# A decode step with two cached-attention layers: tiles of two heads with 64 KB rows in three fixed places, and VectorE's products stored before they are summed

## The chip, the cores and the metric

The kernel runs on one core of one Trainium2 chip. The metric is the device time of one execution in microseconds. The kernel before took 2550.75 us in the median of three runs (2548.57 to 2551.07).

## What is computed

Two tokens (batch 2, one position each, width 576) pass twice through an attention block and a mixer block, with the same weights both times. In the attention 32 heads of width 128 meet a cache of 16,384 keys and values per head and batch row; all numbers are bf16.

```python
q = (x @ wq).reshape(B, Sq, H, Dh) ...
scores = jnp.einsum("bhqd,bhkd->bhqk", q, k_cache) * (Dh ** -0.5)
p = _softmax(scores, axis=-1)
o = jnp.einsum("bhqk,bhkd->bhqd", p, v_cache)
return o... @ wo
...
x = x + _A_ref(_layernorm(x, axis=-1), A_k_cache, A_v_cache, A_wq, A_wo)
x = x + _B_ref(_layernorm(x, axis=-1), B_w1, B_w2, B_w3, B_w4)
x = x + _A_ref(_layernorm(x, axis=-1), A_k_cache, A_v_cache, A_wq, A_wo)
x = x + _B_ref(_layernorm(x, axis=-1), B_w1, B_w2, B_w3, B_w4)
```

With one position the shifts in the mixer read padding only, so `@ w2` multiplies zeros. Nearly all bytes are the caches: 64 pairs of batch row and head, each with 4 MiB of keys and 4 MiB of values, are read once per layer, except a few that stay on the chip between the layers.

## The kernel before, in words

**Tiles.** A unit `u` is one head of one batch row (64 units per layer). Its keys are one tile, its values another: 128 partitions by 32,768 bytes, that is 128 positions per partition, one contiguous run of 32 KB per partition (`plan_tile`). SBUF holds six such places (`NSLOT`, `TILE`), which the tiles of K and V take in a ring. In front of them lie 6,144 bytes for three transposed chunks (`AUX`) and a small gap (`EXTRA`).

**Order of the transfers.** `plan_all` lists every load of the program in one order: K of unit 0, the weights wq and w2, then K and V alternating (V one unit behind K), then the weights of the tail of layer 0 cut to fit a window of freed bytes (`WINDOW`), then layer 1 alike. All loads are issued by SyncE (SP) in that order; `Store.pump` issues the next as soon as the program has released all the bytes that it overwrites, and SP waits (L98, L182) for the engines' semaphores that say so. A tile's bytes are released 512 at a time (`used`), but a whole tile is loaded by one DMA, so the last reader of the old tile decides. When a tile has landed, GpSimd passes the news to TensorE and VectorE (`landed`; POOLq L187 in the profile).

**One unit.** Of a unit's 128 blocks of 128 keys, 64 go to TensorE and 64 to VectorE (`PB`). TensorE takes eight blocks at a time (`CH`): it transposes them into one of four PSUM banks (`transposed`, L1255), ScalarE copies the bank to SBUF (`evacuate`, L1270), and two chunks later (`LEAD`) TensorE multiplies the eight transposed blocks by the query column (`scores`, L1285). VectorE multiplies 16 blocks by the query spread over all partitions into `prod` and sums them at once (`dots`, L1315 and L1319), four times per unit. Then come the maxima (L1324, L1330, L1332), a maximum over the partitions on GpSimd (L1335), two exponentials with their sums (L1345, L1349), and 128 matmuls of the values with the probabilities, which accumulate one column (`pv`, L1375).

**The loop.** In `attention` a loop's turn is three units (`NS`), 21 turns per layer. Within a unit `s` the engines also do the maximum and the exponentials of unit `s-1` and its `pv`. Each engine runs its own loop; `HEAD` gives the place in the instruction stream at which TensorE's loop begins. What lies before and after the loop is written out.

**Between the layers.** Layer 1 begins with the units that layer 0 ended with, in another order, so that three K tiles and two V tiles (`HELD`, `CARRY`) and 13,824 bytes of a third V (`PART`) need no second load. While the weights of layer 0's tail pass through the window, TensorE transposes the keys of the first unit of layer 1 in place (`ahead`, `lay`), and layer 1 starts with scores straight from them (`early_scores`, L1300). At the end of a layer `last_head` does the last unit and multiplies by wo (L956); `two_norms`, the w3 columns (L882), the w4 groups (L956) and `finish` follow.

Of the kernel before, what the change touches and what calls it, by code (L numbers as in the profile page):

```python
# [32 lines left out]
class Graph:  # L33
# [79 lines left out]
    def column(self, ap, s):  # L113
        if self.shift is None:
            return ap[:, s:s + 1]
        return ap[:, bass.ds(self.shift + s, 1)]
# [149 lines left out]
CELL = 128  # L266
# [72 lines left out]
class KB:  # L339
    NL = 2  # L340
    CH = 8
    LEAD = 2
    HOLD = 4
    TILE = 32768
    NSLOT = 6
    CARRY = 2
    HELD = 3
# [4 lines left out]
    PB = 32  # L352
# [11 lines left out]
    }  # L364
    PART = 13824
    REST = [(13824, 8192), (22016, 8192), (30208, 2560)]
    HEAD = (200, 60)
    EC = 96

    def __init__(self, nc, A_x, K, V, wq, wo, w1, w2, w3, w4, out):  # L370
# [12 lines left out]
        self.NB = S // 128  # L383
        self.BP = self.NB // 2
        assert self.BP == 64 and self.F % 128 == 0 and D == 576 and all(sum(x) == self.MT for x in self.GROUPS)
# [5 lines left out]
        self.chunk = self.made = self.turn = 0  # L391
# [3 lines left out]
        ch, pb, bp = self.CH, self.PB, self.BP  # L395
        self.early = ([(h, b, 2 * pb + h * (bp - pb) + b - pb) for h in range(2) for b in range(pb, bp, ch)] +
                      [(h, b, h * pb + b) for h in range(2) for b in range(0, pb, ch)][self.HOLD:])
# [4 lines left out]
    def _alloc(self):  # L402
# [6 lines left out]
        self.kt = [self.mem[:, i * w:(i + 1) * w].rearrange("p (i c) -> p i c", c=128) for i in range(self.NKT)]  # L409
# [3 lines left out]
        self.qb = [sb(f"qb{i}", [128, 128], BF16) for i in range(self.NS)]  # L413
        self.p = [sb(f"p{i}", [128, self.NB], BF16) for i in range(self.NS)]
        self.s_dve = [sb(f"s_dve{i}", [128, 2 * (self.BP - self.PB)], FP32) for i in range(self.NS)]
        self.q_f = sb("q_f", [128, U + 1], BF16)
        self.q_col = sb("q_col", [128, self.NS], BF16)
        self.mx = sb("mx", [128, 5, self.NS], FP32)
        self.l1 = sb("l1", [128, U], FP32)
        self.l2 = sb("l2", [128, U], FP32)  # L420
        self.o_acc = sb("o_acc", [128, U + 1], FP32)
# [3 lines left out]
        share = self.s_dve[1][:, :].bitcast(BF16)  # L425
# [45 lines left out]
    def plan_tile(self, T, t, u, slot, cuts=None):  # L471
        b, hh = u % self.B, u // self.B
        src = T[b, hh].rearrange("(p j) d -> p (j d)", p=128)
        if cuts is None:
            self.store.plan((t, u), f"tile{slot}", self.slot(slot), self.TILE, [(lambda m: m, src)])
            return
        self.parts[t, u] = self.slot(slot), [lo for lo, n in cuts] + [0] * ((t, u) == self.partly())
        for lo, n in cuts:
            self.store.plan((t, u, lo), f"part{slot}_{lo // 4096}", self.slot(slot) + lo, n,
                            [(lambda m: m, src[:, lo // 2:(lo + n) // 2])])  # L480

    def partly(self):

        return "v", self.U - self.CARRY - 1

# [45 lines left out]
    def plan_all(self):  # L531
# [9 lines left out]
        place = [(i + 2) % 6 for i in range(len(tiles))]  # L541
        place[-1] = 4
        full = lambda k, m, at: (k, 0, m, at)
        hd, mt = self.H, self.MT
        for i, (t, u) in enumerate(tiles):
            self.plan_tile(source[t], t, u, place[i])
            if i == 0:
                self.store.plan(None, "xin", 0, 0, [(self.rows[0:B, :], self.A_x.rearrange("b s d -> (b s) d"))], ["prod"])
                self.plan_cols("wq", 0, self.wq, [full(k, hd, s[0] + wqr * k) for k in range(self.KT)])
                self.plan_small("w2", 0, self.w2, s[0] + wqr * (self.KT - 1) + wqr // 2, (0, 64))  # L550
# [12 lines left out]
        ring = [i if i < 2 else (i + 1) % 6 for i in range(len(tiles))]  # L563
        for i, (t, u) in enumerate(tiles):
            q = self.TILE // 4
            cuts = (self.REST, [(q * j, q) for j in (0, 1, 3, 2)], [(q * j, q) for j in (0, 2, 1, 3)])[i] if i < 3 else None
            self.plan_tile(source[t], t, u, ring[i], cuts)
        assert ring[-6:] == [4, 5, 0, 1, 2, 3]
        self.plan_heads(1, [s[4], s[4] + r8, s[4] + 2 * r8, s[5], s[4] + 3 * r8])
        a = s[5] + row * self.WO_CUT  # L570
        self.plan_small("w1", 1, self.w1, a, (0, 64))
        a += row * self.KT
        self.plan_cols("w3", 1, self.w3, [full(0, mt, a), full(1, mt, a + w3r), full(2, mt, s[0]), full(3, mt, s[0] + w3r),
                                          full(4, mt, s[0] + 2 * w3r)])
        assert a + 2 * w3r <= self.size
        b = s[0] + 2 * w3r + w3r // 2
        assert b + g[0] <= s[1]
        self.plan_groups(1, [b, s[1], s[1] + g[1], s[1] + g[1] + g[2], s[1] + 3 * g[1], s[1] + 4 * g[1], s[2], s[2] + g[6]], CELL)

    def order(self, l):  # L580
        U = self.U
        return list(range(U)) if l == 0 else [U - 1, U - 3, U - 2] + list(range(U - 3))

    def runs(self, l):

        U = self.U
        return [(0, 0, U)] if l == 0 else [(0, U - 1, 1), (1, U - 3, 2), (3, 0, U - 3)]

    def held(self):

        U = self.U
        return {("k", u) for u in range(U - self.HELD, U)} | {("v", u) for u in range(U - self.CARRY, U)}

    def tile_order(self, l):
# [3 lines left out]
        for s in range(self.U + 1):  # L598
            if s < self.U and ("k", o[s]) not in have:
# [29 lines left out]
    def build(self):  # L629
# [10 lines left out]
        for t, k in ((self.x, "x"), (self.st[:, 1, :, :], "st1"), (self.st[:, 2, :, :], "st2"), (self.xb[:, :, :], "xb"),  # L640
                     (self.x1[:, :, :], "x1"), (self.hs[:, :, :], "hs"), (self.zero[:, :, :], "zero"),
                     (self.xn[:, :, :], "xn"), (self.xn2[:, :, :, :], "xn2"),
                     (self.q_f[:, :], "q_f")):
            self.pool(lambda e, t=t: e.memset(t, 0.0), writes=[k])
        def f(e):
# [45 lines left out]
    def ahead(self, l, n):  # L691
# [3 lines left out]
        for _ in range(n):  # L695
            u = self.order(1)[0]
            c = len(self.held_over)
            if c < self.HOLD:
                at = self.chunk + len(self.early) + c
                self.held_over.append((0, u, c, at))  # L700
                self.transposed(u, c * self.CH, ("t", c), at % self.NT)
                self.used(1, "k", u, c * self.CH, self.CH)
            elif self.made < len(self.early):
                h, b, col = self.early[self.made]
# [3 lines left out]
                self.laid.append((h * self.BP + b, i))  # L708
                self.transposed(u, h * self.BP + b, None, i, True)

    def lay(self, l, n):
# [3 lines left out]
        for _ in range(n):  # L715
            if not self.laid:
                return
            b0, i = self.laid.pop(0)
            nm, buf, keys = self.tile("k", self.order(1)[0], b0, self.CH)
            self.act(lambda e, buf=buf, i=i: e.activation(out=buf, in_=self.sps[i][:, :].bitcast(BF16), func=ACT.Copy),  # L720
                     reads=[("sps", i), ("qps", i)], writes=keys, to="tensor")
# [182 lines left out]
    def q_projection(self, l):  # L904
# [3 lines left out]
        if l:  # L908
            at = self.order(l)[0]
            self.dv(lambda e: e.tensor_copy(out=self.q_col[:, 0:1], in_=q[:, at:at + 1]),  # L910
# [552 lines left out]
```

## Time and profile before

| | us |
|---|---|
| median of three runs | 2550.75 |
| lowest and highest | 2548.57, 2551.07 |
| span of the profiled execution, first to last instruction | 2549.0 |

The profiled execution is shown by its span alone; the median of the runs is 1.75 us above it. Views used in the prediction: the page (busy share of each engine, 40 slices with the DMA engines' share and GB/s, the DMA queues, the issues by size), the table by stretch, the timeline, the chain of waits and SP's own waits. In the timeline a row gives the start, the time from the first to the last instruction that it merges, the engine, the line, the operation with its tiles, and how many instructions; in brackets the idle time before and what ended it. SPq rows are DMA issues.

### The profile page before, as it was taken

The page shows a single profiled execution, that of the slowest core. Times are in us where ns is not written, and L with a number is a line of the kernel's source. Part 1 is how long each engine was busy: PE and PEld are TensorE (multiplying, and loading weights), DVE is VectorE, ACT ScalarE, POOL GpSimd, SP SyncE. Part 2 cuts the span into 40 slices and gives each one's busy share as a digit, 9 for nine tenths or more (in the row PEclk, how much of TensorE's full clock was granted, in tenths as well). Part 3 has the DMA queues.
Part 4 walks back from the last instruction along what each step waited for, and adds up shares of the span by engine and source line. Part 5 has one row for each costly group of instructions (what it writes and reads, how often), then busy time and mean ns, then how long its engine had stood idle before and what let it go on. Part 6 is the DMA issues. An engine that isn't in the chain of part 4 may idle for free.

```text
span 2549.0 us, 75293 instructions
## 1 busy us (share of the span) xinstructions
PE 1523.7 (60%) x34486; PEld 1434.2 (56%) x34486; DVE 1875.6 (74%) x1920; ACT 1114.2 (44%) x1833; POOL 164.1 (6%) x161
## 2 busy tenths in 40 slices
PE   4655655655565565556677655555565556556556
PEld 4555555555555455555677655555555555555555
DVE  5877776777777777777649877777677777767773
ACT  3434443443444344344346444444444344434432
POOL 0000000000000000000000000000000000000000
PEclk8666666666666666666657666666666666666665
DMA  9999999999999999999999999999999999999999
GB/s 413 427 435 429 435 429 435 429 434 430 433 431 431 432 431 433 430 433 430 423 403 424 431 433 431 432 432 431 432 431 433 430 433 430 433 430 433 430 433 381
DMA packets 46498, 1093.00 MB, mean 429 GB/s; under 512 B 5114, under 2 KB 6780, under 8 KB 11516
## 3 DMA queue, kind: packets, MB, share of 16 engines
q1 hardware_dynamic: 46460, 1092.46, 100.0%
q8 instruction: 28, 0.46, 0.1%
q14 instruction: 10, 0.08, 0.0%
HBM read 1092.44 MB, written 0.00 MB: 429 GB/s over the span
## 4 chain that ended last, share of the span: by engine, by line
DMA 70%; DVE 20%; issue 8%; PE 1%; SPq 0%; POOLq 0%; DVEq 0%; ACT 0%
DMA mem<-in_A_k_cache_dram 64%; DVE s_dve L1319 9%; DVE prod L1315 9%; DMA mem<-in_B_w_dram 2%; DMA mem<-in_A_wo_dram 2%; DMA mem<-in_A_v_cache_dram 1%; DVE mx L1324 0%; SPq L98 0%; DVE mx L1332 0%; DMA mem<-in_A_wq_dram 0%; DVE q_col L1201 0%; DVE o_acc L1356 0%; DVE mx L1330 0%; PE tps L1255 0%; PE sps L882 0%
## 5 line engine op out<-in xcount | busy, mean ns | idle before, releaser
L1270 ACT ACTIVATE mem<-tps 128x1024 bf16<-128x1024 bf16 x1020 | 958.3, 1036 | 1296.0 <-PE tps L1255 1289.9
L1255 PE MATMUL tps<-ident,mem 128*128 128x128 bf16 x8160 | 813.3, 271 | 708.6 <-POOLq L187 708.1
L1319 DVE TENSOR_REDUCE s_dve<-prod 128x16 f32<-128x2048 bf16 x508 | 1161.3, 2286 | 17.4
L1255 PEld LDWEIGHTS tps<-ident,mem 128*128 128x128 bf16 x8160 | 669.2, 124 | 718.6 <-POOLq L187 717.7
L1315 DVE TENSOR_TENSOR prod<-mem,qb 128x2048 bf16<-128x2048 bf16 x508 | 620.9, 1222 | 537.1 <-POOLq L187 530.5
L1375 PE MATMUL mps<-p,mem 128*128 128x1 bf16 x16384 | 450.6, 165 | 84.5 <-POOLq L187 74.6
L1375 PEld LDWEIGHTS mps<-p,mem 128*128 128x128 bf16 x16384 | 443.1, 102 | 99.8 <-ACT p L1349 98.7
L1285 PE MATMUL sps<-q_col,mem 128*128 128x1 bf16 x8160 | 369.2, 166 | 159.1 <-ACT mem L1270 142.9
L1285 PEld LDWEIGHTS sps<-q_col,mem 128*128 128x128 bf16 x8160 | 320.7, 101 | 216.4 <-ACT mem L1270 211.8
L1335 POOL PARTITION_ALL_REDUCE mx<-mx x128 | 160.2, 1251 | 2332.4 <-DVE mx L1332 2332.4
L1345 ACT ACTIVATE p<-s_dve,mx 128x64 bf16<-128x64 f32 x128 | 44.5, 348 | 15.5
L1214 ACT ACTIVATE qb<-sps 128x128 bf16<-128x128 f32 x129 | 34.0, 263 | 24.3 <-PE sps L1211 24.3
L1211 PE MATMUL sps<-ident,q_col 128*128 128x128 bf16 x129 | 29.7, 230 | 15.6 <-DVE q_col L1201 15.6
L1349 ACT ACTIVATE p<-sps,mx 128x64 bf16<-128x64 f32 x128 | 37.5, 293 | 0.0
L1343 ACT ACTIVATE mx<-mx 128x1 f32<-128x1 f32 x128 | 30.6, 239 | 12.3 <-POOL mx L1335 12.3
L1324 DVE TENSOR_REDUCE mx<-s_dve 128x1 f32<-128x64 f32 x128 | 28.2, 220 | 4.5
L882 PE MATMUL sps<-xn,mem 128*128 128x2 bf16 x544 | 21.3, 173 | 13.6 <-DMA mem<-in_A_wq_dram 7.3
L882 PEld LDWEIGHTS sps<-xn,mem 128*128 128x128 bf16 x544 | 20.0, 119 | 14.9 <-DMA mem<-in_A_wq_dram 8.1
L1330 DVE TENSOR_REDUCE mx<-sps 128x1 f32<-128x64 f32 x128 | 27.4, 214 | 0.7 <-DVEq L259 0.7
L1356 DVE COPY o_acc<-mps 128x1 f32 (+1 forms) x130 | 19.4, 149 | 7.5 <-PE mps L1375 7.5
L1349 ACT ACTIVATION_READ_ACCUMULATOR p<-sps,mx (+1 forms) x128 | 24.2, 189 | 0.0
L1345 ACT ACTIVATION_READ_ACCUMULATOR p<-s_dve,mx (+1 forms) x128 | 23.8, 186 | 0.0
(108 smaller groups left out, 235.0 us busy)
## 6 DMA issues: line engine op xcount, KB each, us to landing
mem<-in_A_v_cache_dram SPq DMA_DIRECT2D x125, 4096.0 KB, 45.5
mem<-in_A_k_cache_dram SPq DMA_DIRECT2D x123, 4096.0 KB, 43.2
mem<-in_A_wq_dram SPq DMA_DIRECT2D x8, 1024.0 KB, 11.5
mem<-in_A_k_cache_dram SPq DMA_DIRECT2D x8, 1024.0 KB, 8.0
mem<-in_B_w_dram SPq DMA_DIRECT2D x14, 576.0 KB, 6.8
mem<-in_B_w_dram SPq DMA_DIRECT2D x7, 864.0 KB, 21.4
mem<-in_B_w_dram SPq DMA_DIRECT2D x4, 1152.0 KB, 16.6
mem<-in_A_wo_dram SPq DMA_DIRECT2D x6, 576.0 KB, 10.0
```

The source lines that it names most:

```text
L882: ins = pe.matmul(out[:, m * B:(m + 1) * B], lhsT=buf[:, c:c + 127 * d + 1:d], rhs=self.xn[:, k, :], start=first and m == lo, stop=False, ...
L1214: self.act(lambda e: e.activation(out=self.qb[s % self.NS][:, :], in_=qps, func=ACT.Copy), reads=[("qps", i)], writes=[("qb", s % self.NS) ...
L1255: ins = pe.transpose(out[:, j * 128:(j + 1) * 128], buf[:, j * 128:(j + 1) * 128], self.ident[:, :])
L1270: self.act(lambda e: e.activation(out=self.kt[k], in_=self.tps[t][:, :].rearrange("p (i c) -> p i c", i=self.CH), func=ACT.Copy), reads=[( ...
L1285: ins = pe.matmul(self.sps[sp][:, c * self.CH + j:c * self.CH + j + 1], lhsT=self.kt[k][:, j, :], rhs=self.q_col[:, sp:sp + 1], start=True ...
L1315: self.dv(lambda e: e.tensor_tensor(out=prod, in0=buf.rearrange("p (j d) -> p j d", d=128), in1=qbc, op=ALU.mult), reads=[("qb", s % self. ...
L1319: self.dv(lambda e: e.tensor_reduce(out=sd[:, c0:c0 + DB], in_=prod, axis=AX.X, op=ALU.add), reads=["prod"], writes=[("s_dve", s % self.NS ...
L1335: self.pool(lambda e: e.partition_all_reduce(self.mx[:, 3, m:m + 1], self.mx[:, 2, m:m + 1], channels=128, reduce_op=ROP.max), reads=[("mx ...
L1343: self.act(lambda e: e.activation(out=self.mx[:, 4, m:m + 1], in_=self.mx[:, 3, m:m + 1], func=ACT.Copy, scale=-self.scale), reads=[("mx3" ...
L1345: self.act(lambda e: e.activation(out=p[:, n:self.NB], in_=self.s_dve[s % self.NS][:, :], func=ACT.Exp, bias=self.mx[:, 4, m:m + 1], scale ...
L1349: self.act(lambda e: e.activation(out=p[:, 0:n], in_=self.sps[i][:, 0:n], func=ACT.Exp, bias=self.mx[:, 4, m:m + 1], scale=self.scale, acc ...
L1375: ins = pe.matmul(self.mps[:, 448:449], lhsT=buf[:, j * 128:(j + 1) * 128], rhs=p[:, col:col + 1], start=(h == 0 and b == 0), stop=(h == 1 ...
```

## The change

- A tile is now a pair of heads of one batch row: partitions 0 to 63 hold the first head, 64 to 127 the second, 65,536 contiguous bytes each (`plan_tile`, `TILE`). There are three places instead of six: V always loads into the first, K into the second, and the third (C) takes the second K tile at a layer's start and its last V, and in between the products of VectorE and two more transposed chunks.
- A loop's turn is one pair: 29 turns in layer 0 and 28 in layer 1. In it VectorE first multiplies all four parts of 32 blocks (`product`) into place C and later sums them (`gather`); the next query is spread after two of the four sums. TensorE transposes 16 chunks with five PSUM banks and five places for transposed chunks, and the scores follow four chunks behind (`FAR`). Then come the scores' end, the `pv` of the pair before, the maximum and the exponentials of this pair. Before, product and sum alternated, and maximum and exponentials belonged to the unit before.
- Scores and values have two columns per matmul (both queries); maxima and exponentials run on halves of 64 partitions, and the one maximum over partitions has two columns. There is one `p`, one query column and one set of scores in the loop, where there were three.
- The first two and the last pairs of layer 0, and the first three and the last of layer 1, are written out (`unit`), with 16 blocks per VectorE step; in four of them TensorE takes 160 of 256 blocks (`PB_ENDS`) instead of 128, and `pv` of the pair before is woven between the chunks (`behind`).
- Held over to layer 1: one K tile, one V tile and 46,592 bytes of a second V. The offsets of the weights' window move by 32,768 bytes. At the start wq and w2 are loaded before the first K. The last V of layer 0 comes in three parts.

```diff
-    TILE = 32768
-    NSLOT = 6
+    FAR = 4
+    TILE = 65536
+    NSLOT = 3
-    PB = 32
+    DM = 32
+    PB = 64
+    PB_ENDS = 80
-    HEAD = (200, 60)
+    LAST_V = [(0, 32768), (32768, 16384), (49152, 16384)]
...
-        src = T[b, hh].rearrange("(p j) d -> p (j d)", p=128)
+        src = T[b, 2 * j:2 * j + 2].rearrange("h (p j) d -> (h p) (j d)", p=self.HALF)
...
-            self.plan_tile(source[t], t, u, place[i])
+            self.plan_tile(source[t], t, u, C if i == 1 or last else A if t == "k" else V, self.LAST_V if last else None)
...
+        self.plan_tile(source["v"], *tiles[0], V, self.REST)
+        self.plan_tile(source["k"], *tiles[1], A, [(q * j, q) for j in range(4)])
+        self.plan_tile(source["k"], *tiles[2], C, [(2 * q * j, 2 * q) for j in range(2)])
...
+            lead, nt, nkt = (self.FAR, self.NT + 1, self.FAR + 1) if steady else (self.LEAD, self.NT, self.NKT)
...
+            if steady:
+                for x in parts:
+                    self.product(l, s, o[s], *x)
+                self.tick()
+            for i, c in enumerate(chunks):
+                t, k = i % nt, i % nkt
+                self.transposes(l, s, o[s], c, t, stay)
...
+                    self.evacuate(t, k)
+                if len(pend) > lead:
+                    self.scores(*pend.pop(0))
+                if not steady and i % every == 0 and i // every < len(parts):
+                    self.dots(l, s, o[s], *parts[i // every])
+                while weave and weave[0][0] == i:
+                    weave.pop(0)[1]()
             while pend:
                 self.scores(*pend.pop(0))
+            if steady:
+                for x in parts[:2]:
+                    self.gather(l, s, *x)
+                q_next()
+                for x in parts[2:]:
+                    self.gather(l, s, *x)
+            self.first_max(l, s)
...
+                for g in range(4):
+                    self.pv(l, s - 1, o[s - 1], g)
+            if not final:
+                if s:
+                    self.keep_o(s - 1)
+                self.softmax_max(l, s)
+                self.softmax_exp(l, s)
...
+            self.q_broadcast(l, 0)
+            unit(0)
+            unit(1, behind(0, 6, 2))
...
+            unit(1, behind(0, 3, 1, True))
+            unit(2, behind(1, 4, 2))
...
-        self.g.loop(first, (U - 1) // NS, NS, self.HEAD[l])
+        for s in range(lo, hi):
+            unit(s)
+        self.g.loop(first, hi - lo, 2, None)
+        self.store.release("far")
+        unit(hi)
...
+    def product(self, l, s, u, h, i):
...
+        self.dv(lambda e: e.tensor_tensor(out=prod, in0=buf.rearrange("p (j d) -> p j d", d=128), in1=qbc, op=ALU.mult),
+                reads=self.spilt(("qb", m)) + self.lands(nm[:2], b0, n, 1) + keys, writes=pk, to="vector")
+        self.used(l, "k", u, b0, n)
+
+    def gather(self, l, s, h, i):
...
+        self.dv(lambda e: e.tensor_reduce(out=sd[:, c0:c0 + n], in_=prod, axis=AX.X, op=ALU.add),
+                reads=pk, writes=self.spilt(("s_dve", m)), to="vector")
...
+                ins = pe.matmul(self.mps[:, 448:450], lhsT=buf[:, j * 128:(j + 1) * 128],
+                                rhs=self.p[:, col, :], start=(h == 0 and b == 0),
```

More of the change, by code (lines that the diff above doesn't have):

```diff
@@ L575, in plan_all @@
[L575 to L578, printed above, removed]
+        self.plan_cols("w3", 1, self.w3, [full(k, mt, a + w3r * k) for k in range(self.KT)])
+        a += w3r * (self.KT - 1) + w3r // 2
+        assert a % CELL == 0 and a + sum(g) <= self.size
+        self.plan_groups(1, [a + sum(g[:i]) for i in range(len(g))], CELL)
@@ L1134, in attention @@
-        self.g.loop(first, (U - 1) // NS, NS, self.HEAD[l])
+                    self.scores(l, 0, o[0], held[0][0], 0, False, False)
+                    self.evacuate(held[3][1], 0)
+            w, h = len(self.early) * CH, self.HALF
+            for i in range(2):
+                self.dv(lambda e, i=i: e.tensor_copy(out=self.s_dve[1][i * h:(i + 1) * h, 0:w],
+                                                     in_=self.mps[i * h:(i + 1) * h, i:2 * w:2]),
+                        reads=["mps"], writes=self.spilt(("s_dve", 1)), to="vector")
@@ L1283, in f, with scores @@
+    def scores(self, l, s, u, c, k, here, last):
+        sp = self.ix(l, s)
+        n = self.CH
+        if here:
+            nm, buf, keys = self.tile("k", u, self.block(l, s, c), n)
+            kt = buf.rearrange("p (i c) -> p i c", c=128)
+        else:
+            kt, keys = self.kt[k], self.kt_keys(k)
         def f(pe):
-            for j in range(self.CH):
-                ins = pe.matmul(self.sps[sp][:, c * self.CH + j:c * self.CH + j + 1], lhsT=self.kt[k][:, j, :],
-                                rhs=self.q_col[:, sp:sp + 1], start=True, stop=True, skip_group_check=True)
@@ L1287, in f @@
[L1287 to L1289 removed]
+            for j in range(n):
+                b = 2 * (c * n + j)
+                ins = pe.matmul(self.sps[sp][:, b:b + 2], lhsT=kt[:, j, :],
+                                rhs=self.q_col[:, 2 * sp:2 * sp + 2], start=True, stop=True, skip_group_check=True)
+            return ins
+        self.pe(f, reads=[("q_col", sp)] + keys, writes=[("sps", sp)], sig=("s", c, k, sp),
```

528 lines of the change are left out of this document (292 added, 236 removed), and 8 rows, old and new, of the table WINDOW.

## The prediction

> **What bounds the kernel now.** I read the page first: busy shares, the 40 slices, the DMA queues, the chain of waits, the sizes of the issues.
>
> ```profile
> span 2549.0 us, 75293 instructions
> ...
> PE 1523.7 (60%) x34486; PEld 1434.2 (56%) x34486; DVE 1875.6 (74%) x1920; ACT 1114.2 (44%) x1833; POOL 164.1 (6%) x161
> ...
> DMA  9999999999999999999999999999999999999999
> GB/s 413 427 435 429 435 429 435 429 434 430 433 431 431 432 431 433 430 433 430 423 403 424 431 433 431 432 432 431 432 431 433 430 433 430 433 430 433 430 433 381
> ...
> q1 hardware_dynamic: 46460, 1092.46, 100.0%
> q8 instruction: 28, 0.46, 0.1%
> ...
> DMA 70%; DVE 20%; issue 8%; PE 1%; SPq 0%; POOLq 0%; DVEq 0%; ACT 0%
> ...
> mem<-in_A_v_cache_dram SPq DMA_DIRECT2D x125, 4096.0 KB, 45.5
> mem<-in_A_k_cache_dram SPq DMA_DIRECT2D x123, 4096.0 KB, 43.2
> ```
>
> The 16 DMA engines are busy for 100.0% of the span, and no compute engine for more than 74%. The 20% for DVE in the chain of waits is bookkeeping: the DMA of a K tile is issued when VectorE has let go of the place, but 43.2 us pass until it lands, so several transfers of that size stand in line ahead of it. The table by stretch shows three kinds of stage: the loop, the weights between the layers, and the start of layer 1.
>
> ```profile
> 1000.00:1058.29 58.29, 34.13 (x777) 32.21 (x775) 43.69 (x43) 25.45 (x42) 3.76 (x3) 0.65 1.00 432
> ...
> 1262.60:1313.00 50.40, 36.52 (x845) 33.59 (x845) 7.85 (x52) 19.13 (x26) 0.00 (x0) 0.51 1.01 397
> 1313.00:1371.20 58.20, 48.28 (x1118) 45.74 (x1119) 53.55 (x59) 36.42 (x60) 5.01 (x4) 0.68 1.00 414
> ```
>
> A turn of three units takes 58.29 us (columns: PE, PEld, DVE, ACT, POOL busy, granted clock, DMA share, GB/s). **So the kernel is its DMA packets laid end to end.** The change can gain only by cheaper packets, and lose wherever the queue runs dry.
>
> **Term 1: fewer packets.** A packet's cost besides its bytes comes from two cadences in the timeline, both set by landings: the transposes of successive K tiles (16 packets of 32 KB per engine apart: one K and one V), and the steps of the w3 columns (1152 KB each, 8 packets of 9,216 bytes per engine).
>
> ```profile
> 1008.96 2.74 PE L1255 MATMUL tps<-ident,mem 128*128 128x128 bf16 x24 [6.17 <-POOLq L187]
> ...
> 1028.40 2.74 PE L1255 MATMUL tps<-ident,mem 128*128 128x128 bf16 x24 [6.08 <-POOLq L187]
> ...
> 2523.78 1.72 PE L882 MATMUL sps<-xn,mem 128*128 128x2 bf16 x36 [0.29 <-DMA mem<-in_B_w_dram]
> 2526.57 1.72 PE L882 MATMUL sps<-xn,mem 128*128 128x2 bf16 x36 [1.07 <-DMA mem<-in_B_w_dram]
> 2529.34 1.73 PE L882 MATMUL sps<-xn,mem 128*128 128x2 bf16 x36 [1.05 <-DMA mem<-in_B_w_dram]
> 2532.18 1.72 PE L882 MATMUL sps<-xn,mem 128*128 128x2 bf16 x36 [1.11 <-DMA mem<-in_B_w_dram]
> ```
>
> 19.44 us / 16 = 1215 ns per 32 KB; (2529.34 - 2523.78) / 16 = 347.5 ns per 9,216 bytes. The line through both has 867.5 / 23,552 = 0.03683 ns per byte and 347.5 - 339.4 = 8 ns per packet. The wq steps before layer 1 (8 packets of 8,192 bytes) give 2.49 us / 8 = 311 ns, and with the 32 KB packets 0.03678 ns per byte and 10 ns per packet.
>
> ```profile
> 1306.80 0.93 PEld L882 LDWEIGHTS sps<-xn,mem 128*128 128x128 bf16 x32 [0.40 <-DMA mem<-in_A_wq_dram]
> ...
> 1309.29 0.93 PEld L882 LDWEIGHTS sps<-xn,mem 128*128 128x128 bf16 x32 [1.55 <-DMA mem<-in_A_wq_dram]
> ```
>
> I take 9 ns, which includes a packet's share of the semaphore writes. K and V now come in 248 x 128 = 31,744 packets of 32 KB; whole pairs make 122 x 128 = 15,616 of 64 KB, and with the tiles that are cut at the hand-over K and V lose about 16,000 packets. The bytes are equal (held over: 5 x 32,768 + 13,824 = 2 x 65,536 + 46,592 per partition). Gain: 16,000 x 9 ns / 16 engines = **-9.0 us**. Bounds: 0, if a run of 64 KB still travels as two packets; -17, if K and V came at 435 GB/s, the fastest slice on the page, instead of 432 (1040 MB / 432 - 1040 MB / 435).
>
> A page speaks for a smaller gain: the Trainium skill, DMA: Bandwidth & Descriptors, section Why small descriptors are slow, gives a packet a fixed three cycles and 32 bytes of descriptors. At the 850 MHz of that page this is an estimate of 4.7 ns and -4.7 us instead of -9.0, which would bring the time to 2549. The rows above measure 8 and 10 ns, so the sum keeps 9.
>
> **Term 2: does the loop keep the queue fed?** Two places now alternate, so K of the next pair can only be issued when this pair's K has been read, and must be there when V (half a turn, 19.43 us = 58.29 / 3) has passed. Count from the landing of K:
>
> ```profile
> 1009.08 1.23 DVE L1315 TENSOR_TENSOR prod<-mem,qb 128x2048 bf16<-128x2048 bf16 x1 [4.63 <-POOLq L187]
> 1010.03 7.65 ACT L1270 ACTIVATE mem<-tps 128x1024 bf16<-128x1024 bf16 x8 [10.82 <-PE tps L1255]
> 1010.34 2.29 DVE L1319 TENSOR_REDUCE s_dve<-prod 128x16 f32<-128x2048 bf16 x1
> ...
> 1012.56 0.40 PE L1285 MATMUL sps<-q_col,mem 128*128 128x1 bf16 x8
> ...
> 1012.82 1.01 PE L1255 MATMUL tps<-ident,mem 128*128 128x128 bf16 x8
> ...
> 1013.11 1.25 POOL L1335 PARTITION_ALL_REDUCE mx<-mx  x1 [18.18 <-DVE mx L1332]
> ...
> 1013.63 0.40 PE L1285 MATMUL sps<-q_col,mem 128*128 128x1 bf16 x8
> ...
> 1018.76 3.55 PE L1375 MATMUL mps<-p,mem 128*128 128x1 bf16 x128 [0.54 <-ACT p L1349]
> ...
> 1032.02 0.61 PE L1255 MATMUL tps<-ident,mem 128*128 128x128 bf16 x8
> ```
>
> - VectorE: four products of twice the size, 4 x 2 x 1.23 = 9.8 us. The sums, 8 x 2.29 = 18.3, come afterwards and hold no key.
> - TensorE and ScalarE: the first eviction starts 1.07 us after the first transpose (1008.96 to 1010.03), each takes 7.65 / 8 = 0.956. With five banks chunk 15 waits for eviction 10: 1.07 + 11 x 0.956 = 11.6, plus its transposes 0.61 to 1.01: **12.6 us**.
> - Issue to landing with nothing in line: the output's DMA, SP's own wait below, 0.9 us, with the issue itself 1.2. So the next K flows 13.8 us after the landing at the latest; it is due at 19.4. Slack 5.6 us; cost 0.
> - V: its two-column matmuls I price like one-column ones (2 x 3.55 = 7.1); they end at 26.5, and the place is due at 38.9. At w3's two-column rate (1.72 / 36 = 48 ns) they would end at 31.7, still in time.
> - VectorE per turn: 43.69 x 2/3 = 29.1 of 38.9 us; the maxima start near 29, GpSimd's 1.25 and four exponentials end near 33. ScalarE's next eviction is due at 39. The cover is V's transfer; every microsecond beyond 19.4 would cost 57 us in 57 turns.
>
> ```profile
> SPq L212 <- DMA out_dram<-prod: 0.9, 1, 0.9
> ...
> SPq L182 <- DVE mx L1324: 1431.7, 121, 17.3
> SPq L98 <- PE sps L1285: 845.0, 125, 19.1
> ```
>
> The added wait stands on SP, where it already waits 1431.7 and 845.0 us in sum; behind it in SP's order only V of the same pair is queued, whose place comes free later anyway.
>
> **Term 3: the start.** wq now goes ahead of K, behind the small load of x: the first wide transfer is issued 0.46 us later (the second issue instead of the first; rows below): **+0.5**. The first pair's keys are done about 20 us after they land, while two more 8 MB tiles are in transfer: no gap.
>
> ```profile
> 0.79 0.41 SPq L98 DMA_DIRECT2D mem<-in_A_k_cache_dram  x1
> 1.25 0.32 SPq L98 DMA_DIRECT2D prod<-in_A_x_dram  x1
> ```
>
> **Term 4: instruction loads.** Much more is written out (TensorE some 3,800 matmuls outside the loops, before some 600). The 28 instruction packets of 16 KB may double: 0.46 MB at 432 GB/s is **+1** us spread over the engines, at most +17 if all fell on one of them.
>
> **Term 5: the hand-over.** The weights' window has its old size and order: 397 GB/s stays. The start of layer 1 loses 58.2 x (1 - 414 / 432) = 2.4 us today. After it, counted from the last wq (1313.0): V's rest ends at 5.6, K of the second pair at 25.0, then K(0) 44.4, K(1) 63.8, V(0) 83.2. VectorE's two written-out pairs take 6 and 8 steps of 3.53 us: from 15.3 (second quarter landed) to 36.5, and, after the second pair's maximum near 41, to 69.3. Spreading q, maximum, GpSimd and four exponentials, which ScalarE must do before the next evictions, end near 74.7; eleven evictions and the transposes bring K(1)'s release to 85.8, K(2) flows at 87.0: 3.8 us after V(0) has passed, once. With 0.6 for V(0), whose place also comes late, 4.4 - 2.4 = **+2** (bounds -2.4 and +8).
>
> **Term 6: the end.** The last V is a pair: 3.55 us more of pv behind it. The waits for w3 quoted above (0.29 + 1.07 + 1.05 + 1.11 = 3.52) take it up, so 0; without them +3.5.
>
> Sum: -9.0 + 0.5 + 1 + 2 = -5.5, a span of 2543.5; the median of the runs stands 1.75 above the span: **2545.2**, said as 2545.
>
> **The rivals.** *No cheaper packets* (two packets per run, or a cost that goes with the bytes): 2545 + 9 = 2554. For it: no row shows a packet above 32 KB. Against: three packet sizes lie on one line with 8 to 10 ns. *The refill of K comes late in every turn*, which ends slower: the first transposes run at the low clock (1.01 for eight, a chunk every 1.07 us, 1012.56 to 1013.63), and granted clock in the loop is 0.65. At that pace the release is 5 x 0.91 + 11 x 1.07 = 16.3, still in time; it decides from 18.2. If two-column scores at the low clock cost half as much again (pitch 1.27): 18.5, 0.3 us late, x 57 turns = +17: 2562. Against: today the pace reaches 0.61 within 5 us of the landing, and eviction at 0.956 then leads. *Slower HBM reads*: rows start 64 KB apart instead of 32 and the two halves of the partitions 4 MB apart; if the engines met in the same part of memory and K and V fell to the 414 GB/s of the third stretch, 1040 MB would take 105 us more: 2650. No row shows such a conflict. The Trainium skill, DMA: Bandwidth & Descriptors, section Latency and other measured facts, measured a loss from 214 to 207 GB/s at rows 512 KiB apart, an estimate of 80 us here; no run here shows it. *All of the headroom gained* (435 GB/s): 2537.
>
> **How the numbers follow.** About 0.2% (5.1 us: below 2545.6 or above 2555.9) is what a measurement of this kernel can tell from no change. Forecast 0.52 (its own range 2540 to 2550: faster 0.42, same 0.10); no cheaper packets 0.19 (all within); late refill 0.20 and slower HBM 0.05 (slower); full headroom 0.04 (faster). Faster 0.46, same 0.29, slower 0.25. The range 2537 to 2562 leaves out the slow reads and the worse half of the late refills.
>
> **What would show it.** Right: packets near 30,000, a loop turn near 38.72 us (58.29 x 2/3 less 16 x 9 ns), a K issue 12 to 14 us after the landing, one gap of some microseconds at the start of layer 1. Wrong: as many 32 KB packets as now; slices of the loop below 432 GB/s; a DMA share below 100% with SP waiting for L1255 or the products past V's landing; or more than one gap between the layers.

## The result, and the profile after

The changed kernel took **2965.87 us** (2963.73 to 2966.51) against 2550.86 us for the kernel before in the same session: ratio 1.1627, 95% interval 1.1611 to 1.1643. It is 16% slower, 421 us above the forecast and far outside its range. The profiled execution has a span of 2964.3 us, 415.3 us more than before. First the page of the changed kernel:

```profile
span 2964.3 us, 74226 instructions
...
DMA  9988898988988889888899889898888888988889
GB/s 415 380 384 354 354 393 343 396 353 341 395 354 368 371 351 394 354 355 383 368 371 392 354 354 382 352 389 348 354 382 354 382 354 354 396 344 363 382 364 378
...
q1 hardware_dynamic: 28460, 1092.45, 86.8%
q8 instruction: 49, 0.80, 0.1%
...
DMA 68%; ACT 21%; PE 6%; issue 3%; SPq 1%; another core or an unknown queue 1%; DVE 0%; POOLq 0%; POOL 0%; ACTq 0%; DVEq 0%
```

The packets are fewer, as the change says (28,460 on the load queue instead of 46,460), and carry the same bytes. But the DMA engines are busy for 86.8% instead of 100.0%, evenly over all slices: the loss is in every turn of the loop, not at the seams. The chain now spends 21% of the span on ScalarE, which was not on it before. One turn of the loop, in the table by stretch (columns: PE, PEld, DVE, ACT, POOL busy, granted clock, DMA share, GB/s):

```profile
1006.90:1052.70 45.80, 21.21 (x514) 20.28 (x514) 27.73 (x15) 17.14 (x26) 0.36 (x1) 0.61 0.86 366
```

Two units took 38.86 us before; a turn takes 45.80 now. 57 turns x 6.94 = 396 of the 415 us. No engine is busy for more than 27.73 us of it, so no engine became the bound. The same turn in the timeline:

```profile
1007.04 3.60 PE L1363 MATMUL tps<-ident,mem 128*128 128x128 bf16 x32 [12.37 <-POOLq L187]
1007.18 8.90 DVE L1447 TENSOR_TENSOR mem<-mem 128x4096 bf16<-128x4096 bf16 x4 [11.45 <-POOLq L187]
...
1010.43 1.06 PE L1363 MATMUL sps<-ident,mem 128*128 128x128 bf16 x8
1011.28 0.40 PE L1401 MATMUL sps<-q_col,mem 128*128 128x2 bf16 x8
...
1011.71 0.33 SPq L98 DMA_DIRECT2D mem<-in_A_v_cache_dram  x1
...
1019.66 0.33 SPq L98 DMA_DIRECT2D mem<-in_A_k_cache_dram  x1
...
1033.50 6.99 PE L1524 MATMUL mps<-p,mem 128*128 128x2 bf16 x256 [8.13 <-POOLq L187]
...
1052.84 3.60 PE L1363 MATMUL tps<-ident,mem 128*128 128x128 bf16 x32 [12.35 <-POOLq L187]
```

K lands at 1006.95 (the chain below). The next K is issued at 1019.66, 12.7 us later, for the forecast's 12.6. What is wrong is the other row: **the next V is issued only at 1011.71**, 4.8 us after K has landed. `pv` (L1524), the last reader of V's place, ended at 1040.5 in the turn shown, and the V that replaces it is issued at 1057.50, 17 us later and again 4.7 us behind the landing of a K. Until V is issued the queue is empty, since K's refill stands behind it in SP's order: in the trace's DMA records the last packet of the landed K ends at 1006.59 and the first of the next V starts at 1012.68. What SP waits for says which instruction let it go:

```profile
SPq L98 <- PE sps L1401: 2388.9, 119, 38.0
SPq L182 <- DVE sc L1239: 266.2, 57, 15.4
SPq L98 <- PE mps L1524: 48.3, 4, 24.3
```

V's place is released by a `scores` (L1401), which reads keys and not values, and not by `pv` (L1524), for which SP waits four times in the whole program, against 57 turns. In the timeline it is the first `scores` of a turn, at 1011.28, and with the scores four chunks behind (`FAR`) that one stands after five chunks of transposes of a K that has just landed. The chain of waits goes from one K to the next in each turn:

```profile
973.98 32.97 DMA mem<-in_A_k_cache_dram
...
1007.04 1.05 PE tps L1363 x8
...
1008.12 11.11 ACT mem L1381 x12
...
1019.28 0.37 PE sps L1401 x8
...
1019.66 33.09 DMA mem<-in_A_k_cache_dram
```

K takes 33 us from issue to landing because V, issued 8 us before it, is in transfer: the chain's ScalarE share is K's release, which V's transfer would have covered, had V been issued in time.

**Why a score.** A semaphore (the counter by which one engine tells another that it is done) of this program is from one engine to one other, or general. An operation whose result is meant for one engine (`to="vector"`, `to="scalar"`) raises only that engine's semaphore; when SP too depends on it, SP is given the next operation behind it that raises the general one:

```python
    def _stand_in(self, o, d):
        if d.sem is not None or d.to is None or d.to == o.eng:
            return d
...
        x = next(x for x in self.ops[d.eng][d.pos + 1:] if x.to is None and not x.relay)
```

The last group of `pv` is for VectorE, the transposes that follow it are for ScalarE, so the next general operation of TensorE is the next turn's first `scores`.

### The profile page after: what moved, and what is told of

Read it like the earlier page. It is cut to its first block, busy times and chain, and to the rows that moved or that the text cites. A ratio compares the mean times of both kernels' runs of the same rounds, so it can differ in the third digit from the quotient of the medians.

```text
span 2964.3 us, 74226 instructions
## 1 busy us (share of the span) xinstructions
PE 1430.3 (48%) x34641; PEld 1340.5 (45%) x34641; DVE 1763.9 (60%) x1125; ACT 1128.6 (38%) x1707; POOL 28.9 (1%) x100
## 2 busy tenths in 40 slices
DMA packets 28518, 1093.33 MB, mean 369 GB/s; under 512 B 3114, under 2 KB 4780, under 8 KB 9516
## 3 DMA queue, kind: packets, MB, share of 16 engines
q1 hardware_dynamic: 28460, 1092.45, 86.8%
## 4 chain that ended last, share of the span: by engine, by line
DMA 68%; ACT 21%; PE 6%; issue 3%; SPq 1%; another core or an unknown queue 1%; DVE 0%; POOLq 0%; POOL 0%; ACTq 0%; DVEq 0%
DMA mem<-in_A_k_cache_dram 65%; ACT mem L1381 21%; PE tps L1363 3%; DMA mem<-in_A_v_cache_dram 2%; DMA mem<-in_B_w_dram 1%; SPq L98 1%; PE mps L1524 1%; PE sps L1401 1%; DMA mem<-in_A_wq_dram 0%; PE sps L1363 0%; PE sps L916 0%; PE sps L1008 0%; PE sps L1417 0%; ACT p L1499 0%
## 5 line engine op out<-in xcount | busy, mean ns | idle before, releaser
L1381 ACT ACTIVATE mem<-tps 128x1024 bf16<-128x1024 bf16 x837 | 813.8, 1091 | 604.9 <-PE tps L1363 601.3
L1457 DVE TENSOR_REDUCE s_dve<-mem 128x32 f32<-128x4096 bf16 x228 | 1007.1, 4417 | 3.9
L1363 PE MATMUL tps<-ident,mem 128*128 128x128 bf16 x6792 | 609.0, 251 | 720.8 <-POOLq L187 717.7
L1447 DVE TENSOR_TENSOR mem<-mem 128x4096 bf16<-128x4096 bf16 x228 | 507.1, 2286 | 622.3 <-POOLq L187 622.3
L1363 PEld LDWEIGHTS tps<-ident,mem 128*128 128x128 bf16 x6792 | 496.8, 115 | 723.3 <-POOLq L187 723.3
L1524 PE MATMUL mps<-p,mem 128*128 128x2 bf16 x16384 | 449.4, 165 | 508.4 <-POOLq L187 490.3
L1524 PEld LDWEIGHTS mps<-p,mem 128*128 128x128 bf16 x16384 | 443.1, 104 | 520.0 <-POOLq L187 483.2
L1401 PE MATMUL sps<-q_col,mem 128*128 128x2 bf16 x8192 | 360.8, 165 | 158.3 <-ACT mem L1381 135.3
L1401 PEld LDWEIGHTS sps<-q_col,mem 128*128 128x128 bf16 x8192 | 303.0, 98 | 223.7 <-ACT mem L1381 211.7
L1381 ACT ACTIVATE mem<-sps 128x1024 bf16<-128x1024 bf16 x171 | 191.1, 1117 | 0.0
L1436 DVE TENSOR_REDUCE s_dve<-prod 128x16 f32<-128x2048 bf16 x42 | 96.0, 2286 | 2.0 <-ACT p L1493 0.6
L1482 POOL PARTITION_ALL_REDUCE mx<-mx x64 | 24.3, 380 | 2877.2 <-DVE mx L653 2877.2
## 6 DMA issues: line engine op xcount, KB each, us to landing
mem<-in_A_k_cache_dram SPq DMA_DIRECT2D x4, 2048.0 KB, 12.7
```

Of the source, the lines that this page charges most:

```text
L1363: ins = pe.transpose(out[:, j * 128:(j + 1) * 128], buf[:, j * 128:(j + 1) * 128], self.ident[:, :])
L1381: self.act(lambda e: e.activation(out=self.kt[k], in_=src.rearrange("p (i c) -> p i c", i=self.CH), func=ACT.Copy), reads=bk, writes=self. ...
L1401: ins = pe.matmul(self.sps[sp][:, b:b + 2], lhsT=kt[:, j, :], rhs=self.q_col[:, 2 * sp:2 * sp + 2], start=True, stop=True, skip_group_chec ...
L1436: self.dv(lambda e: e.tensor_reduce(out=sd[:, c0:c0 + DB], in_=prod, axis=AX.X, op=ALU.add), reads=["prod"], writes=self.spilt(("s_dve", m ...
L1447: self.dv(lambda e: e.tensor_tensor(out=prod, in0=buf.rearrange("p (j d) -> p j d", d=128), in1=qbc, op=ALU.mult), reads=self.spilt(("qb", ...
L1457: self.dv(lambda e: e.tensor_reduce(out=sd[:, c0:c0 + n], in_=prod, axis=AX.X, op=ALU.add), reads=pk, writes=self.spilt(("s_dve", m)), to= ...
```

## The experiments

The theory: V's place is free when `pv` ends but is reported by the next turn's first `scores`, so in a loop with one place for V the queue runs dry in every turn. The rivals: that the place really is needed that long; that two places for K and V are too few whatever is reported; and that packets of 64 KB are slow. Line numbers shift by a few between the kernels.

**A signal of its own behind pv.** One transpose of the identity (nobody reads its result) that raises the general semaphore:

```diff
                 for g in range(4):
                     self.pv(l, s - 1, o[s - 1], g)
+                if steady:
+                    self.token()
...
+    def token(self):
+        self.pe(lambda pe: pe.transpose(self.tps[1][:, 0:128], self.ident[:, :], self.ident[:, :]), reads=["ident"],
+                writes=[("tps", 1)], sig=("token",))
```

> The changed kernel with one small transpose into a free PSUM bank right after a loop turn's pv; it computes nothing that is used, but gives SP a signal of its own that V's place is free. Theory (V's refill waits for the next turn's first scores, because SP's wait goes to the next TensorE instruction that signals to everyone): V is issued within 1 us of the end of pv instead of 17 us later, the gap of 7.1 us per turn goes, a loop turn takes 38.7 to 38.9 us instead of 45.8, and the time falls by about 57 x 7.1 = 400 us to 2545 to 2570. Rival (two alternating places are too few, whatever signals them): the turn stays above 43 us and the time above 2800.

Measured: 2560.35 us (2558.09 to 2563.95), ratio to before 1.0046 (1.003 to 1.0063). One small instruction takes back 405 us. A turn of this kernel by stretch and in the timeline:

```profile
1000.00:1038.70 38.70, 21.08 (x520) 19.42 (x516) 27.73 (x16) 17.15 (x27) 0.35 (x1) 0.65 1.00 434
```

```profile
1038.83 0.33 SPq L98 DMA_DIRECT2D mem<-in_A_k_cache_dram  x1
...
1045.57 6.99 PE L1531 MATMUL mps<-p,mem 128*128 128x2 bf16 x256 [1.03 <-POOLq L187]
...
1052.42 0.27 PE L1508 MATMUL tps<-ident 128*128 128x128 bf16 x1
1052.72 0.33 SPq L98 DMA_DIRECT2D mem<-in_A_v_cache_dram  x1
```

The DMA share is 1.00 again, the turn 38.70 us at 434 GB/s. V is issued 0.2 us after `pv` has ended, 13.9 us behind K, while K is still in transfer. SP now waits for the added transpose, once in each of the 57 turns:

```profile
SPq L98 <- PE tps L1508: 772.0, 57, 14.5
```

The place was not needed any longer, and two alternating places are enough for the loop.

**The same signal, later.** To see that the time follows the moment of the signal and not the added instruction, it is moved behind the first chunk of the next turn.

```diff
+                if steady and i == 0:
+                    self.token()
...
-                if steady:
-                    self.token()
```

> The same small transpose, but in the next turn, after its first chunk of transposes. Theory: the signal that frees V's place comes about 1.2 us after the landing of K instead of 4.7, so each turn is shorter by 3.5 us (42.3 us) and the time is 2966 - 57 x 3.5 = 2765. Rival (two places too few): as without it, 2966.

Measured: 2784.64 us (one run). V is issued 1.3 us after K has landed, and the turn lies between the other two:

```profile
1041.97:1084.73 42.76, 20.86 (x515) 19.13 (x515) 27.74 (x16) 17.19 (x27) 0.35 (x1) 0.64 0.93 395
```

The turn shown is 4.06 us above the full queue. Over all turns of the loop, K lands every 42.5 us on average and V is issued 1.3 us after that; in the changed kernel it is 45.85 and 4.6 us, and a turn with a full queue takes 38.7. So the turn falls by 3.3 us where the wait falls by 3.3: each microsecond of the wait costs one. On top come 2.5 us in both kernels. The DMA records of both show what they are, as averages over their turns and the 16 DMA engines: the landing is reported 0.6 us after an engine's last packet has ended, the first packet of V starts 1.2 us after the issue, and it takes some 0.65 us longer than the 2.42 us of the packets behind it. The expectation of 2765 was 20 us low: it reckoned 3.5 us per turn, of which 3.3 came, and some 9 us more were lost outside the loop's turns, for a cause that stays open.

**The signal in the kernel before.** The edit is the same `token` behind `pv` in the loop of before.

> The kernel before with the same small transpose after pv in its loop. Theory: there too V's place is freed by a later score, but several transfers stand in line, so an earlier issue changes nothing: 2551, within 0.2%; issue to landing of V grows by some microseconds. Rival (the late signal costs in the kernel before as well): below 2545.

Measured: 2549.51 us, ratio 1.0 (0.999 to 1.0009). SP's waits for a `scores` and the time of a V from issue to landing, in this run:

```profile
SPq L98 <- PE sps L1286: 19.0, 10, 5.6
...
mem<-in_A_v_cache_dram SPq DMA_DIRECT2D x125, 4096.0 KB, 52.5
```

The 125 waits for a `scores` have become 10, and V is issued earlier (52.5 us before its landing, 45.5 in the kernel before), yet the time is the same. So the kernel before has the same late report, and it costs nothing there: with six places several transfers stand in line (43 to 45 us from issue to landing in the page of before), so a place reported late is still reported early enough. The change made no signal later in its order; it took away the line that hid it.

**Product and sum alternating in the loop.** The signal stays, but VectorE works as before, 16 blocks multiplied and summed at a time, and place C holds only the two transposed chunks in the loop.

```diff
-            size = self.DM if steady else self.DB
+            size = self.DB
...
-                for x in parts:
-                    self.product(l, s, o[s], *x)
...
-                if not steady and i % every == 0 and i // every < len(parts):
+                if i % every == 0 and i // every < len(parts):
...
-                for x in parts[:2]:
-                    self.gather(l, s, *x)
```

> The run with the signal of its own after pv, and VectorE in the loop multiplying and summing 16 blocks at a time in alternation, as before the change, instead of all products first. Theory: K's place is then free 28.5 us after its landing instead of 12.6, K flows about 31 us after it and is due at 19.4, so a turn takes about 50 us and the time is near 2550 + 57 x 11.5 = 3200. Rival (the order on VectorE does not matter): the time of the run with products first.

Measured: 3276.33 us (one run). By stretch and in the timeline:

```profile
1000.21:1051.50 51.29, 21.12 (x515) 19.73 (x515) 29.46 (x23) 17.14 (x26) 0.35 (x1) 0.60 0.77 327
```

```profile
1022.50 1.23 DVE L1425 TENSOR_TENSOR prod<-mem 128x2048 bf16<-128x2048 bf16 x1 [13.27 <-POOLq L187]
1023.76 2.29 DVE L1429 TENSOR_REDUCE s_dve<-prod 128x16 f32<-128x2048 bf16 x1
...
1047.56 1.23 DVE L1425 TENSOR_TENSOR prod<-mem 128x2048 bf16<-128x2048 bf16 x1
...
1051.50 0.33 SPq L98 DMA_DIRECT2D mem<-in_A_k_cache_dram  x1
```

VectorE's work per turn is nearly the same (29.46 and 27.73 us busy), but the last product ends 26 us after the first begins instead of 8.9, and K's refill leaves 29 us after the landing instead of 12.7. It is due at 19.4, so it is 9.6 us late; with the 2.5 us that an empty queue costs on top that is 12.1 of the 51.29 - 38.70 = 12.6. The expectation of about 3200 was low because it took a turn of about 50 us. So two alternating places work only with the products ahead of the sums, as the change has them.

**The relay for the held V, earlier.** The own signal leaves 2560 where the forecast had 2545. Its trace loses most of the rest at the start of layer 1, where three transfers land 9.1, 5.6 and 1.3 us later than they would right behind the transfer before. The row for the first of them, in the kernel with the own signal:

```profile
1336.85 1.85 PE L1531 MATMUL mps<-p,mem 128*128 128x2 bf16 x64 [11.62 <-POOLq L187]
...
1341.50 0.33 SPq L98 DMA_DIRECT2D mem<-in_A_k_cache_dram  x1
```

TensorE waits 11.62 us for GpSimd's news that the V held since layer 0 is there. It had long been there; but GpSimd passes news on in order, and this one stands behind those for the four parts of the second K, of which the last landed at 1336.5. The edit gives it ahead of them:

```diff
+                if not exp:
-                self.landed("v", o[s], False)
+                    self.landed("v", o[s], False)
...
+            self.landed("v", o[0], False)
             unit(1, behind(0, 3, 1, True))
```

> Own signal as in e1_own_signal, and GpSimd's relay for the V held since layer 0 is moved ahead of the four relays for the parts of layer 1's second K. If that relay's place in GpSimd's order is what held PE at the hand-over, K(0) into place C is issued about 8 us earlier than in e1 (about 1333 instead of 1341.5 us), its gap of 9.1 us shrinks to about 1 us or none, V(0)'s gap of 5.6 us shrinks with it, and the time is 2545 to 2552 us (e1: 2560). If the hand-over is bound by something else (the chain of scores and exponentials, or the engine order of PE), the issue stays near 1341 us and the time near 2560.

Measured: 2554.63 us (2552.62 to 2556.92), ratio to before 1.0018 (1.0009 to 1.0028). The wait is gone, and `pv` now follows the probabilities:

```profile
1330.16 1.77 PEld L1533 LDWEIGHTS mps<-p,mem 128*128 128x128 bf16 x64 [3.07 <-ACT p L1503]
1330.17 1.85 PE L1533 MATMUL mps<-p,mem 128*128 128x2 bf16 x64 [2.98 <-ACT p L1503]
```

K(0) is issued at 1334.82 instead of 1341.50 and lands without a gap. But 5.7 us came back, not 9: the three transfers behind it now lose 3.0, 6.0 and 2.9 us. (The profiled execution of this kernel took 2556.92 us, 2.3 above its median, so its gaps are on the large side.) The relay was one cause of several.

**The same kernel with 32 KB packets.** It measures the first term of the forecast by itself: each row of 64 KB is loaded in two halves of 32 KB, by two DMAs.

```diff
-            self.store.plan((t, u), f"tile{slot}", self.slot(slot), self.TILE, [(lambda m: m, src)])
+            w = self.TILE // 4
+            self.store.plan((t, u), f"tile{slot}", self.slot(slot), self.TILE,
+                            [(lambda m, i=i: m[:, i * w:(i + 1) * w], src[:, i * w:(i + 1) * w]) for i in range(2)])
```

> As e6_early_relay, but every row of 64 KB is loaded as two transfers of 32 KB, so that the packets are those of before. If fewer packets are cheaper as the prediction's first term has it, the loop's turn is about 38.86 us instead of 38.70 and the time about 9 us above e6 (57 turns of 0.16 us). If packets of 64 KB are no cheaper, the turn and the time are those of e6.

Measured: 2561.42 us (2560.22 to 2562.02), 6.8 above the kernel with 64 KB packets. One turn of each, K issue to K issue, first with 64 KB and then with 32 KB:

```profile
1000.77:1039.49 38.72, 20.98 (x515) 19.27 (x515) 27.74 (x16) 17.15 (x27) 0.35 (x1) 0.65 1.00 433
```

```profile
1003.87:1042.72 38.85, 20.98 (x515) 19.25 (x515) 27.73 (x16) 17.14 (x27) 0.36 (x1) 0.65 1.00 432
```

The landings of successive turns stand 38.70 and 38.86 us apart: 0.16 us for 16 packets per engine, 10 ns each, 9.1 us in 57 turns. About 1 ns of the 10 belongs to the second DMA of each tile: its 4-byte packet on each engine takes 9 ns in the trace. In the profiled executions the start of layer 1 loses some 2 us less with the smaller transfers, and so the whole differs by 6.8.

**The rest at the start of layer 1.** In the unit before the loop of layer 1 (`unit(2)`, counted from 0; the expectation calls it the second) the `pv` groups are woven between the chunks, and the next V is issued when the last of them has ended (1383.42 in the kernel with the early relay). They are moved forward:

```diff
-            unit(2, behind(1, 4, 2))
+            unit(2, behind(1, 3, 1))
```

> As e6_early_relay, and in the second unit of layer 1 the four groups of V(1)'s matmuls stand behind chunks 3, 4, 5 and 6 instead of 4, 6, 8 and 10. In e6 the next V was issued at 1383.42 us, when the last of these groups (ended 1382.3) had let go of its place, and landed 25.39 us after the transfer before it, 6.0 us more than a transfer takes. If the place of these groups in PE's order is what made that V late, it is issued 4 to 6 us earlier, the gap falls to 0 to 2 us and the time by 4 to 6 us, to about 2549. If PE is held there by something else (its instruction supply, the evacuations), issue and time stay as in e6 (2554.6).

Measured: 2554.66 us, ratio 1.0018 (1.0009 to 1.0027): no change. V was issued at 1378.54, 4.9 us earlier, as expected, and its gap fell from 6.0 to 2.5 us. The gap of the K behind it rose from 2.9 to 5.0: part of the gap moved to the next transfer, which was issued only 1.5 us earlier.

> As e8_weave_earlier, and in layer 0 the groups of V(0) stand behind chunks 4 to 7 instead of 6, 8, 10 and 12. e6 lost 1.5 and 0.8 us there, to a V issued at 93.17 us. If that order is the cause, 1 to 2 us less than e8; if V(0)'s landing (76.3 us) is, no change against e8.

With `behind(0, 4, 1)` in layer 0 as well: 2555.69 us, ratio 1.0029 (1.0017 to 1.004). The V there was issued 0.2 us earlier (92.69 for 92.92), the K behind it later (116.18 for 113.02). Nothing gained. In both kernels the first group starts at V(0)'s landing, at 76.3 us. The groups then stand closer together, but TensorE stands still between them for 1.7 and 3.1 us, in waits that the profile puts down to nothing but issue, and the last group ends at 91.6 (91.8 without the edit).

**Less for VectorE in the same unit.** In that unit of layer 1 VectorE is busy without a gap until 1388.6 us, and only then begins the loop's first products. Here it leaves out 30 of its 128 blocks of scores in this one unit of layer 1.

```diff
+        w = 1 if l and s == 2 and i == 3 else DB
-        self.dv(lambda e: e.tensor_tensor(out=prod, in0=buf.rearrange("p (j d) -> p j d", d=128),
+        self.dv(lambda e: e.tensor_tensor(out=prod[:, 0:w], in0=buf.rearrange("p (j d) -> p j d", d=128)[:, 0:w],
```

> As e8_weave_earlier, and the last of the four parts that VectorE multiplies and sums for each half in the third unit of layer 1 does one block instead of sixteen (30 of 256 blocks of scores of one unit of one layer are left out, which the output shows). In e8 VectorE worked on that unit without a gap from 1357 to 1388.4 us and only then began the first loop turn's products, whose end released the place of the next K (issued 1402.84, 23 us after the K before it landed, against 12.7 us in a settled turn; that K landed 24.32 us after the transfer before it, 5.0 us late). If VectorE's share of that unit is what is left of the loss, that K is issued about 6.5 us earlier and is no longer late, and the time falls by 4 to 5 us, to about 2550. If not, issue and time stay as in e8 (2554.7).

Measured: 2554.36 us, ratio 1.0015 (1.0006 to 1.0024). The idea that VectorE's share of this unit is what holds the next K falls:

```profile
1381.19 0.29 DVE L1474 TENSOR_REDUCE mx<-s_dve 128x1 f32<-128x128 f32 x1
...
1387.69 0.35 PE L1405 MATMUL sps<-q_col,mem 128*128 128x2 bf16 x8 [0.56 <-ACT mem L1385]
1388.08 0.17 DVE L1307 COPY q_col<-q_f 128x2 bf16<-128x2 bf16 x1 [6.59 <-PE sps L1405]
...
1389.44 8.90 DVE L1452 TENSOR_TENSOR mem<-mem 128x4096 bf16<-128x4096 bf16 x4 [0.25 <-POOLq L187]
```

VectorE is done 6 us earlier and waits them out for the last scores: TensorE and ScalarE, which have 16 chunks in this unit (and TensorE four groups of `pv`), end about when VectorE did. The loop's first products begin at 1389.44 instead of 1388.87, and K is again 5 us late. TensorE stands still for 1.2 and 3.1 us in this unit, again in waits put down to issue. What would shorten both engines there was not tried; it stays open whether the changed kernel can be brought below before. None of the versions that ran is faster than the kernel before.

## Why the prediction was wrong, by its steps

- **Term 2, the sentence on V, failed.** It says that the two-column matmuls "end at 26.5, and the place is due at 38.9", and of SP's order that V's "place comes free later anyway". The work was priced right: with the own signal `pv` takes 6.99 us and ends 26.4 us after K's landing. But the step took the end of the last reader for the moment at which SP learns of it. In the changed kernel SP learns of it 17 us later, behind the landing of the next K. Each late turn costs 7 us and there are 57: the term's price of 57 us per microsecond was right, its count of the waits that can be late was not. The row that would have told it was quoted in the prediction: SP waits 845.0 us in 125 waits for L1285, a `scores`. K and V both need a release, and the `pv` line, L1375, has a single wait in that view, in a row that the prediction does not show, below. The prediction does not ask which row is V's release.

```profile
SPq L98 <- PE mps L1375: 7.5, 1, 7.5
```

- **Term 2, K, was right in size, partly by luck**: 12.7 us from landing to issue for 12.6. The forecast took the end of the last transposes, which came earlier than forecast, at 12.2 (1019.18). They too are for ScalarE, and it is again a `scores` behind them that lets SP go (1019.28 to 1019.64, the chain above); here that costs 0.5 us and not 17. The rival of a late K did not happen; a late V, which did, was not among the rivals. Issue to first packet was 1.2 us, as priced. What an empty queue costs beyond it, 1.3 us, was not priced; with V in time it stays covered.
- **Term 1 was right**: 28,518 packets in all for "near 30,000" (2,000 packets of 4 bytes went too, with 125 of the DMAs of K and V), a turn of 38.70 us for 38.72, and 10 ns per packet when each row comes in halves. The rivals of no cheaper packets and of slower reads fall: K and V come at 434 GB/s with rows 64 KB apart. The forecast weighed an estimate of 4.7 ns per packet from the Trainium skill, DMA: Bandwidth & Descriptors, section Why small descriptors are slow; the runs show about twice that.
- **Term 3** was right in its price, a first wide transfer some 0.4 us later. Its "no gap" asked for K alone: with V in time in the loop, the second V of layer 0 lands 1.4 us late and the K behind it 0.2 (own signal; 1.5 and 0.8 with the early relay). **Term 4**: 49 instruction packets for 28, as "may double" had it; but TensorE's stalls of up to 3.5 us in the written-out units, put down to issue, were not priced; whether its instruction supply makes them stays open, since no run here separated it.
- **Term 5 was mis-sized**: +2, with bounds -2.4 and +8, counted from the 2.4 us that the kernel before loses there. With the own signal alone the start of layer 1 loses about 16 us, 12 with the early relay, 9 with the earlier weave, so some 13.6, 9.6 and 6.5 in the term's own count. It assumed that K(0) follows the second K at once. Its place waits for the held V's `pv`, and that waited for a relay queued behind four others. Counted from the last wq, K(0) was forecast at 44.4 us and landed at 54.4 with the own signal alone.
- Without the failed step the sum is roughly borne out: 2545.2 with term 5 at 9.6 instead of 2 is 2552.8, the start of layer 0 adds 1.5 and 0.8, which makes 2555.1, and the kernel with own signal and early relay measures 2554.63. That the two agree so closely is chance: the losses are read from one execution, 2.3 us above the median.

## What to carry to other kernels

When buffers become fewer, ask of each refill not when its last reader ends but which instruction tells the queue so; the waits view names it, and a line that does not read the buffer is a warning. A late report was free here while several transfers stood in line, and cost its whole length and 2.5 us more in each turn when none did. At the start of layer 1 a gap repaired at one transfer partly moved to a later one whose place was late too, so count a seam's loss over all its transfers.

## What the runs showed of the hardware

- A DMA issued into an empty queue cost about 2.5 us of transfer beyond its lateness (7.15 us per turn for an issue 4.6 us after the landing, 3.8 for one 1.3 after it): 0.6 us from an engine's last packet to the landing, 1.2 from the issue to its next packet, and 0.65 in that packet, which took longer than those behind it.
- A maximum over the partitions on GpSimd showed 1.25 us with one column before and shows 0.36 us with two columns in the changed kernel (the profile gives GpSimd's spans only roughly; the reason was not looked for):

```profile
1041.64 0.36 POOL L1482 PARTITION_ALL_REDUCE mx<-mx  x1 [45.46 <-DVE mx L653]
```
